# Linear attention with FP32 projections in the two row halves of TensorE and three groups of three tiles a unit

## The chip, the cores and the metric

One core of one Trainium2 chip. The metric is the device time of one execution in microseconds (us), all of it: attention, then two mixture-of-experts stages in the same program. The change touches the attention stage and, in a few lines, the loading that runs beside it.

## The reference, cut to what is computed

```python
def phi(x):                                   # x: 8 batches, 8 heads, 576 tokens, 64
    proj = einsum('bhsd,df->bhsf', x, w_phi)  # w_phi: 64 x 128
    proj = proj - max(abs(proj), axis=-1)
    return concatenate([exp(proj), exp(-proj)], axis=-1)
q_p, k_p = phi(q), phi(k)
kv = einsum('bhsf,bhsd->bhfd', k_p, v)
z = sum(k_p, axis=2)
out = einsum('bhsf,bhfd->bhsd', q_p, kv) / (einsum('bhsf,bhf->bhs', q_p, z) + 1e-6)
x = out as 4608 tokens x 512
x = (sigmoid(x @ moe_w_gate) * (x @ moe_w_val)) @ moe_w_out     # d_ff 1536
x = moe2(x)            # 8 experts with a capacity of 576 tokens each, assigned in order of the logits
```

All inputs and the output are FP32.

## The kernel before, in words

Attention runs over 16 units. A unit is half the heads of a batch, four heads as two pairs of two (`pr` 0 and 1; `hh` is the head within a pair). With 576 tokens a head, a unit has nine tiles of 128 rows: four full tiles for each pair, and one tile in which the last 64 tokens of both pairs share the 128 rows. The host lays q, k and v out like that.

`GROUPS` cuts the nine tiles into five groups: the shared tile alone, and four groups of two tiles. The loop at the end of `attention` runs over steps `tau`, five to a unit; `at` and `once` start a stage of unit `u` at a fixed number of steps after its first, so that several units are under way at once. The order of the lines in that loop is the order in which the instructions stand in each engine's queue; it is written by hand.

The stages of a unit: 
- `load`, `load_v` (L75, L81): DMAs on SP's queue, k four steps and q four steps ahead of their projection.
- `split` (L89 to L92): x is written as a high part, rounded to FP32R, and the rest as a low part; k's high part on ACT, q's on DVE, low parts on POOL and, for k in two groups of five, on DVE.
- `proj` (L101): per tile three FP32R matmuls (high by high, high by low, low by high), with both heads of the pair in the 128 contraction rows against a block-diagonal `w_phi` of 256 columns. One bank holds a group; three banks are in turn.
- `shift` (L118, L119): on DVE, the largest absolute value of each row of 128, and its subtraction, both read from PSUM.
- `k_exp` (L128): two exps on ACT. `kv_mm` (L148): plain FP32 matmuls of v against them, one head in the upper and one in the lower 64 columns of the array. `z_add` (L156 to L162) on POOL and `z_mm` (L167): the sum over tokens.
- `kv_out`, `kv_tr` (L170 to L177): the result out of PSUM and transposed.
- `q_trL`, `q_tr` (L182, L191): transposes of the shifted q; `q_exp` (L198, L200): exps on ACT and a copy on POOL for the shared tile.
- `q_num`, `q_den` (L212, L231), `q_out`, `den_out`: numerators and denominators, out through ACT to DRAM. `recip` inverts the denominators per batch.

Beside this the loop calls `convert`, which for one chunk of the first expert stage's weights at a time loads 64-bit numbers (`win`, 24 chunks of 512 KB) and turns them into FP32 with five DVE instructions (`to_f32`, L319 to L324), one chunk every three steps.

The next stage, `ffn`, starts while attention ends: `START` says at which steps its generator is advanced. Its `in_mm` (L399) and `out_mm` (L421) are the matmuls of the longest stretch of the program. PSUM has eight banks; attention uses three for `pp`, two for `kv`, and one each for `qt`, `nu` and `misc`, the last shared by `kt`, `lt` and `dn`.

Of the kernel before, what the change touches and what calls it, by code (L numbers as in the profile page):

```python
# [29 lines left out]
GROUPS = ((8, 1), (0, 2), (2, 2), (4, 2), (6, 2))  # L30


K_TAGS = ("k", "kh", "kl", "kpm", "kpmL", "kE", "kEL", "z", "v", "vL")
K_TICKS = 5 * NU + 3


def phi_constants(nc, pool, wphi):

    ones = pool.tile([P, 32], F32, tag="ones", bufs=1, name="ones")
    nc.vector.memset(ones, 1.0)  # L40
    w = pool.tile([P, 2 * F], F32, tag="wphi", bufs=1, name="wphi2")
    nc.vector.memset(w, 0.0)
    nc.sync.dma_start(w[0:D, 0:F], wphi)
    nc.sync.dma_start(w[D:P, F:], wphi)
    hi = pool.tile([P, 2 * F], F32R, tag="whi", bufs=1, name="whi")
    lo = pool.tile([P, 2 * F], F32R, tag="wlo", bufs=1, name="wlo")
    nc.vector.tensor_copy(hi, w)
    nc.vector.tensor_tensor(lo, w, hi.bitcast(F32), op=ALU.subtract)
    return hi, lo, ones


def attention(kctx, qctx, tc, K, wphi, qT, kT, vT, num_d, den_d, r_d, units=NU, extra=None):

# [9 lines left out]
    whi, wlo, ones = phi_constants(nc, qp, wphi)  # L63
# [8 lines left out]
    def load(src, tag, u, j):  # L72
        t0, n = GROUPS[j]
        t = T([2 * P], F32, tag, (u, j), 4)
        nc.sync.dma_start(t[:, : n * P], src[u, :, t0 * P : (t0 + n) * P])  # L75

    def load_v(u, j):
        t0, n = GROUPS[j]
        t = T([n, 2, D], F32, "vL" if n == 1 else "v", (u, j), 2 if n == 1 else 5)
        X["v", u, j] = t  # L80
        nc.sync.dma_start(t.rearrange("p n h d -> p (n h d)"), vT[u, :, t0 * P : (t0 + n) * P])  # L81

    def split(tag, u, j):
        n = GROUPS[j][1] * P
        x = X.pop((tag, u, j))[:, :n]
        h = T([2 * P], F32R, tag + "h", (u, j), 4)[:, :n]
        l = T([2 * P], F32R, tag + "l", (u, j), 4)[:, :n]
        if tag == "k":
            A.activation(h, x, AF.Copy)  # L89
        else:  # L90
            V.tensor_copy(h, x)
        (V if tag == "k" and j in (1, 3) else G).tensor_tensor(l, x, h.bitcast(F32), op=ALU.subtract)  # L92

    def proj(tag, u, j):
        n = GROUPS[j][1]
        pp = psk.tile([P, 2, 2, F], F32, tag="pp", bufs=3, name=f"pp{tag}{u}_{j}")
        h, l = X.pop((tag + "h", u, j)), X.pop((tag + "l", u, j))
        for t in range(n):
            c = slice(t * P, (t + 1) * P)
            for i, (x, w) in enumerate(((h, whi), (h, wlo), (l, whi))):  # L100
                PE.matmul(pp[:, t], lhsT=x[:, c], rhs=w, start=i == 0, stop=i == 2)  # L101
        X["pp" + tag, u, j] = pp

    def shift(tag, u, j):

        n = GROUPS[j][1]
        pp = X.pop(("pp" + tag, u, j))
        m = T([2, 2], F32, "m", (tag, u, j), 4)
        if tag == "k":
            pm = T([n, 2, F], F32, "kpmL" if n == 1 else "kpm", (u, j), 1 if n == 1 else 2)  # L110
            X["kp", u, j] = pm
        elif n == 1:
            pm = T([n, 2, F], F32, "qpmL", (u,), 2)
        else:
            if j % 2:
                T([4, 2, F], F32, "qpm", (u, j // 2), 2)
            pm = X["qpm", u, (j - 1) // 2][:, 2 - 2 * (j % 2) : 4 - 2 * (j % 2)]
        V.tensor_reduce(m[:, 0:n], pp[:, 0:n], axis=AX.X, op=ALU.max, apply_absolute_value=True)  # L118
        V.tensor_tensor(pm, pp[:, 0:n], m[:, 0:n, :, None].to_broadcast([P, n, 2, F]), op=ALU.subtract)  # L119

    def k_exp(u, j):
        n = GROUPS[j][1]
        L, bufs = ("L", 2) if n == 1 else ("", 5)
        E = T([n, 2, 2, F], F32, "kE" + L, (u, j), bufs)
        X["E", u, j] = E
        kp = X.pop(("kp", u, j))
        for s in range(2):
            A.activation(E[:, :, :, s, :], kp, AF.Exp, scale=1.0 - 2.0 * s)  # L128

    def kv_mm(u, j):  # L130

        n = GROUPS[j][1]
        pr = max(j - 1, 0) // 2
        rows = slice(64 * pr, 64 * pr + 64)
        first = j in (0, 3)
        if first:
            X["kv", u, pr] = psk.tile([P, 3, P], F32, tag="kv", bufs=2, name=f"kv{u}_{pr}")
        kv = X["kv", u, pr]
        seq = []
        if first:  # L140
            seq.append((X["v", u, 0][rows, 0], X["E", u, 0][rows, 0]))
        if j > 0:
            seq += [(X["v", u, j][:, t], X["E", u, j][:, t]) for t in range(n)]
        for i, (v, E) in enumerate(seq):
            start, stop = first and i == 0, j in (2, 4) and i == len(seq) - 1
            for hh in range(2):
                o = kv[64 * hh : 64 * hh + 64, 0:2].rearrange("p s f -> p (s f)")
                PE.matmul(o, lhsT=v[:, hh], rhs=E[:, hh].rearrange("p s f -> p (s f)"), start=start, stop=stop)  # L148

    def z_add(u, pr, i):  # L150

        E = X["E", u, 2 * pr + 1 + i].rearrange("p t h s f -> p t (h s f)")
        if i == 0:
            rows = slice(64 * pr, 64 * pr + 64)
            z = T([2, 4 * F], F32, "z", (u, pr), 2)
            G.tensor_tensor(z[:, 0], E[:, 0], E[:, 1], op=ALU.add)  # L156
            L = X["E", u, 0].rearrange("p t h s f -> p (t h s f)")
            G.tensor_tensor(z[rows, 0], z[rows, 0], L[rows], op=ALU.add)
        else:
            z = X["z", u, pr]  # L160
            G.tensor_tensor(z[:, 1], E[:, 0], E[:, 1], op=ALU.add)
            G.tensor_tensor(z[:, 1], z[:, 0], z[:, 1], op=ALU.add)  # L162
# [9 lines left out]
    def kv_tr(u, pr):  # L172
        kt = psq.tile([P, 3, P], F32, tag="misc", bufs=1, name=f"kt{u}_{pr}")
# [5 lines left out]
    def q_trL(u):  # L179
        lt = psq.tile([P, 2, P], F32, tag="misc", bufs=1, name=f"lt{u}")  # L180
        for hh in range(2):
            PE.transpose(lt[:, hh], X["qpmL", u][:, 0, hh], ident)  # L182
        e = T([2, 2, P], F32, "eL", (u,), 2)
        for s in range(2):
            A.activation(e[:, s], lt, AF.Exp, scale=1.0 - 2.0 * s)

    def q_tr(u, h):
        pr, hh = h // 2, h % 2
        tp = psq.tile([P, 4, P], F32, tag="qt", bufs=1, name=f"qt{u}_{h}")
        for j in range(4):  # L190
            PE.transpose(tp[:, j], X["qpm", u, pr][:, j, hh], ident)  # L191
# [62 lines left out]
    def at(f, tau, off, n, *pre):  # L254

        u, i = divmod(tau - off, 5)
        if 0 <= u < units and i < n:
            f(*pre, u, i)

    def once(f, tau, off, *post):  # L260
        u, i = divmod(tau - off, 5)
        if 0 <= u < units and i == 0:
            f(u, *post)

    for tau in range(-5, 5 * units + 10):
        at(load, tau, -4, 5, kT, "k")
        at(load, tau, -2, 5, qT, "q")
        at(load_v, tau, -1, 5)
        once(kv_out, tau, 6, 0)
        once(kv_out, tau, 8, 1)  # L270
        at(proj, tau, 0, 5, "k")
        at(kv_mm, tau, 2, 5)
        once(q_den, tau, 13, 1)
        at(shift, tau, 0, 5, "k")
        at(k_exp, tau, 1, 5)
        once(den_out, tau, 13, 1)
        once(q_den, tau, 11, 0)
        once(z_add, tau, 6, 1, 1)
        once(z_add, tau, 4, 0, 1)
        at(q_num, tau, 8, 4)  # L280
        at(split, tau, -2, 5, "k")
        once(q_trL, tau, 5)
        once(kv_tr, tau, 7, 0)
        once(kv_tr, tau, 9, 1)
        once(den_out, tau, 11, 0)
        at(q_out, tau, 8, 4)
        at(q_tr, tau, 6, 4)
        at(proj, tau, 2, 5, "q")
        at(shift, tau, 2, 5, "q")
        at(q_exp, tau, 6, 4)  # L290
        once(z_mm, tau, 5, 0)
        once(z_mm, tau, 7, 1)
        once(z_add, tau, 3, 0, 0)
        once(z_add, tau, 5, 1, 0)
        at(split, tau, 0, 5, "q")
        once(lambda u: recip_load(u // 2) if u % 2 and u + 1 < units else None, tau, 14)
        once(lambda u: recip(u // 2) if u % 2 and u + 1 < units else None, tau, 16)
# [12 lines left out]
def to_f32(nc, pool, src, dst, name):  # L310
# [5 lines left out]
    def rest():  # L316
        lo, hi = w[:, :, 0], w[:, :, 1]
        a = dst.bitcast(I32)
        V.tensor_scalar(a, hi, 0x7FFFFFFF, None, op0=ALU.bitwise_and)  # L319
        af = a.bitcast(F32)  # L320
# [5 lines left out]
    return rest  # L326
# [8 lines left out]
def ffn(ctx, tc, K, num_d, r_d, wos_d, wout, wg2, w1, w2, wlo_d, x2_d, L, free):  # L335
# [178 lines left out]
    def convert(k):  # L514

        while X["conv"] < min(k, NF):
            X.pop(("rest", X["conv"]))()
# [654 lines left out]
def host(inputs):  # L1172
    import numpy as np

    def xT(x):
# [3 lines left out]
        return np.ascontiguousarray(np.concatenate([a, l], axis=2))  # L1179

    def vt(x):
# [3 lines left out]
        return np.ascontiguousarray(np.concatenate([a, l], axis=2)).reshape(NU, P, 9 * P)  # L1185
# [94 lines left out]
```

## Time and profile before

| | us |
|---|---|
| median of three runs | 1867.48 (1866.4 to 1867.83) |
| profiled execution | 1864.9 |
| its span in the trace | 1863.2 |

| engine | busy, us of the span | share |
|---|---|---|
| PE (matmul) | 1791.2 | 96% |
| PEld (weight load) | 1510.1 | 81% |
| DVE | 1317.5 | 71% |
| ACT | 603.3 | 32% |
| POOL | 610.8 | 33% |

Engines: PE is TensorE, PEld its weight loads, DVE VectorE, ACT ScalarE, POOL GpSimd, SP SyncE, whose queue issues most DMAs. A plain FP32 matmul leaves two records on PE, an FP32R matmul one. The duration that a record of PE shows is modelled and runs on into the records behind it, so what a matmul takes of the engine is read from one start to the next. Transposes are matmuls with one record. The line numbers are those of the kernel before.

### The profile page before, as it was taken

What the parts mean: (1) busy time and instruction counts of PE and PEld (TensorE: products, weight loads), DVE (VectorE), ACT (ScalarE), POOL (GpSimd) and SP (SyncE); (2) the same over time, 40 slices, a digit from 0 to 9 for tenths busy, and PEclk for the clock granted to TensorE, in tenths of its full rate; (3) what the DMA queues carried; (4) which work ended last, traced back from release to release, by engine and by line L of the source; (5) the groups of instructions that cost most, each with busy time, mean ns of one, the idle gap of its engine ahead of it and who ended that gap; (6) DMA issues with size and microseconds to landing.
All of it is one profiled execution on the core that took longest, in us unless ns stands there. A gap on an engine that the chain in (4) does not pass through costs nothing.

```text
span 1863.2 us, 33221 instructions
## 1 busy us (share of the span) xinstructions
PE 1791.2 (96%) x11612; PEld 1510.1 (81%) x11612; DVE 1317.5 (71%) x3242; ACT 603.3 (32%) x1256; POOL 610.8 (33%) x589
## 2 busy tenths in 40 slices
PE   7999999998999999999999999999989999999997
PEld 5665666557899999999999999998667888888886
DVE  8999999859786866857758667454767777777410
ACT  4665665562212222221221221111032333233331
POOL 6766777655322223322332222000211102210121
PEclk9999999999999999999999999999989999999999
DMA  4444444427666676666766666110355645564652
GB/s 140 132 131 131 133 137 135 135 66 257 210 216 212 213 239 224 224 232 212 248 223 216 233 219 216 50 54 12 100 171 181 216 145 174 170 214 147 202 179 87
DMA packets 188118, 318.33 MB, mean 171 GB/s; under 512 B 24240, under 2 KB 67504, under 8 KB 187824
## 3 DMA queue, kind: packets, MB, share of 16 engines
q1 hardware_dynamic: 158448, 254.34, 42.9%
q10 hardware_dynamic: 23616, 43.00, 6.1%
q0 software_dynamic: 5888, 18.88, 2.9%
q8 instruction: 92, 1.51, 0.3%
q14 instruction: 74, 0.61, 0.1%
HBM read 244.53 MB, written 71.60 MB: 170 GB/s over the span
## 4 chain that ended last, share of the span: by engine, by line
PE 65%; DVE 6%; DMA 1%; issue 1%; ACT 0%; SPq 0%; POOLq 0%; POOL 0%; DVEq 0%; ACTq 0%
PE pg L399 28%; PE acc L421 14%; PE hp L1080 11%; PE yp L1114 8%; PE yr L1101 1%; PE tp L1053 1%; PE cnt L801 1%; DMA rb<-r_d 1%; DVE cmp L780 1%; DVE junk L479 1%; DVE oa L987 0%; DMA xg<-x_d,idx 0%; PE lg L455 0%; DVE xl L376 0%; PE num_ix L996 0%
## 5 line engine op out<-in xcount | busy, mean ns | idle before, releaser
L399 PE MATMUL pg<-xl,wh 128*128 128x384 f32 x1152 | 389.5, 338 | 0.9 <-DVE xl L376 0.9
L399 PE MATMUL pg<-xh,wl 128*128 128x384 f32 x1152 | 388.1, 337 | 1.1 <-POOL wl L387 1.1
L399 PE MATMUL pg<-xh,wh 128*128 128x384 f32 x1152 | 387.0, 336 | 0.1
L547 POOL TENSOR_TENSOR el<-er,eh 128x512 fp32r<-128x512 f32 x128 | 182.3, 1424 | 469.2 <-ACT eh L546 431.3
L402 ACT ACTIVATE sg<-pg 128x384 f32<-128x384 f32 x144 | 70.7, 491 | 530.5 <-PE pg L399 514.5
L408 DVE TENSOR_TENSOR sg<-sg,pg 128x384 f32<-128x384 f32 x132 | 72.9, 552 | 228.1 <-PE pg L399 217.3
L399 PEld LDWEIGHTS pg<-xh,wh 128*128 128x128 f32 x1152 | 217.2, 189 | 8.1 <-issue 0.9
L399 PEld LDWEIGHTS pg<-xh,wl 128*128 128x128 f32 x1152 | 215.9, 187 | 6.7 <-POOL wl L387 1.3
L399 PEld LDWEIGHTS pg<-xl,wh 128*128 128x128 f32 x1152 | 216.4, 188 | 1.3 <-DVE xl L376 1.3
L479 DVE SCALAR_TENSOR_TENSOR junk<-x,wg 128x512 f32<-128x512 f32 x240 | 202.1, 842 | 5.5
L421 PE MATMUL acc<-wh,gh 128*128 128x512 f32 x396 | 159.5, 403 | 4.9 <-DVE gh L415 2.7
L421 PE MATMUL acc<-wh,gl 128*128 128x512 f32 x396 | 158.3, 400 | 1.8 <-DVE gl L416 1.7
L421 PE MATMUL acc<-wl,gh 128*128 128x512 f32 x396 | 157.6, 398 | 2.3 <-POOL wl L437 2.2
L1114 PE MATMUL yp<-wh,hh 128*128 128x512 f32 x256 | 108.2, 423 | 0.0
L546 ACT ACTIVATE eh<-er 128x512 fp32r<-128x512 f32 x128 | 81.0, 633 | 75.9 <-POOL el L547 42.4
L1114 PE MATMUL yp<-wh,hl 128*128 128x512 f32 x256 | 100.2, 391 | 0.0
L1114 PE MATMUL yp<-wl,hh 128*128 128x512 f32 x256 | 100.1, 391 | 0.0
L128 ACT ACTIVATE kE<-kpm 128x512 f32<-128x512 f32 x128 | 73.9, 630 | 71.4 <-DVE kpm L119 67.6
L1087 DVE SCALAR_TENSOR_TENSOR hl<-hp,hh 128x288 fp32r<-128x288 f32 (+1 forms) x128 | 54.0, 421 | 60.3 <-ACT hh L1085 60.1
L1080 PE MATMUL hp<-xhT,wh 128*128 128x288 f32 x512 | 94.0, 305 | 0.6 <-ACT xhT L1055 0.5
L1080 PE MATMUL hp<-xhT,wl 128*128 128x288 f32 x512 | 94.3, 301 | 0.0
L421 PEld LDWEIGHTS acc<-wh,gl 128*128 128x128 f32 x396 | 75.0, 190 | 22.3 <-DVE gl L416 4.7
(281 smaller groups left out, 3722.6 us busy)
## 6 DMA issues: line engine op xcount, KB each, us to landing
er<-in_w_dram SPq DMA_DIRECT2D x128, 256.0 KB
wlo_d<-el ACTq DMA_DIRECT2D x128, 256.0 KB
wr<-in_w_dram SPq DMA_DIRECT2D x128, 256.0 KB
wl<-wlo_d SPq DMA_DIRECT2D x128, 256.0 KB
wh<-wos_d SPq DMA_DIRECT2D x120, 256.0 KB
wl<-wos_d SPq DMA_DIRECT2D x120, 256.0 KB
dbli<-in_win_dram SPq DMA_DIRECT2D x24, 512.0 KB
num_d<-nums SPq DMA_DIRECT2D x32, 288.0 KB
```

What stands on the lines that cost most here:

```text
L128: A.activation(E[:, :, :, s, :], kp, AF.Exp, scale=1.0 - 2.0 * s)
L399: PE.matmul(pg, lhsT=a[:, cc], rhs=b, start=c == 0 and j == 0, stop=c == 3 and j == 2)
L402: A.activation(T([TB], F32, "sg", (g,)), X.pop(("pg", g, 0)), AF.Sigmoid)
L408: V.tensor_tensor(u, sg, X.pop(("pg", g, 1)), op=ALU.mult)
L421: PE.matmul(X["acc", i][t], lhsT=a[:, c], rhs=b, start=f == 0 and j == 0, stop=f == NF - 1 and j == 2)
L479: V.scalar_tensor_tensor(junk, x, 1.0, X["wg"][:, e], op0=ALU.mult, op1=ALU.mult, accum_out=out)
L546: A.activation(h, r, AF.Copy)
L547: G.tensor_tensor(tile("el", F32R, k - 1, 3), r, h.bitcast(F32), op=ALU.subtract)
L780: V.tensor_tensor(t[:, c], d[:, c, None, :].to_broadcast([P, NC // 4, NT, 2]), K["it2"][:, None, 0:P:4].to_broadcast([P, NC // 4, NT, 2]), ...
L1080: PE.matmul(hp, lhsT=x[:, cc], rhs=y[:, c, s], start=c == 0 and j == 0, stop=c == 3 and j == 2)
L1087: V.scalar_tensor_tensor(hl[:, s], hs, 0.0, hh[:, s].bitcast(F32), op0=ALU.max, op1=ALU.subtract)
L1114: PE.matmul(yp, lhsT=x[:, cc], rhs=y, start=f == 0 and j == 0, stop=f == 7 and j == 2)
```

## The change

- A unit has three groups of three tiles (`GT`), the shared tile first; the host puts it first too. The loop has three steps a unit, and its lines stand in a new order.
- The splits are gone. `proj` multiplies FP32 by FP32: for each tile two matmuls, one per head, with 64 contraction rows each, head 0 in the upper and head 1 in the lower half of the array's rows. The two heads write to two banks. `pp` has two banks for k and two for q, one set of each.
- `shift` and `k_exp` work on three tiles at once (768 elements a row).
- `kv` has a bank for each pair, which `kt` shares; `lt` shares the bank of `qt`, `dn` that of `nu`. `misc` is gone.
- Loads come two steps ahead of their use, in three DMAs a unit for each of k, q and v.
- `to_f32` gives its five instructions in two parts, three and two, which run one step and two steps after the load; a chunk is started at every second step. `START` and `K_TICKS` are recounted.

```diff
-GROUPS = ((8, 1), (0, 2), (2, 2), (4, 2), (6, 2))
-K_TICKS = 5 * NU + 3
+GT = 3
+K_TICKS = 3 * NU + 2
...
     def load(src, tag, u, j):
+        nc.sync.dma_start(T([GT * P], F32, tag, (u, j), 3), src[u, :, j * GT * P : (j + 1) * GT * P])
...
+    def proj(tag, u, j):
+        pp = psk.tile([P, 2, 512], F32, tag="pp" + tag, bufs=1, name=f"pp{tag}{u}_{j}")
+        x = X.pop((tag, u, j))
+        for t in range(GT):
+            for hh in range(2):
+                r = slice(hh * D, (hh + 1) * D)
+                PE.matmul(pp[:, hh, t * F : (t + 1) * F], lhsT=x[r, t * P : (t + 1) * P], rhs=w[r], start=True, stop=True)
...
+        V.tensor_reduce(m, pp, axis=AX.X, op=ALU.max, apply_absolute_value=True)
+        pm = pm.rearrange("p t h f -> p h t f")
+        V.tensor_tensor(pm, pp, m[:, :, :, None].to_broadcast([P, 2, GT, F]), op=ALU.subtract)
...
+        todo = [[(0, t, slice(0, P)) for t in (1, 2)], [(0, 0, slice(0, P)), (0, 1, slice(0, P))], []][j]
+        if j == 0:
+            todo.insert(0, (0, 0, slice(0, D)))
+        else:
+            todo += [(1, t, slice(0, P)) for t in ((2,) if j == 1 else range(GT))]
+        if j == 1:
+            todo.append((1, None, slice(D, P)))
...
-        kt = psq.tile([P, 3, P], F32, tag="misc", bufs=1, name=f"kt{u}_{pr}")
+        kt = psq.tile([P, 3, P], F32, tag=f"kv{pr}", bufs=1, name=f"kt{u}_{pr}")
...
-        dn = psq.tile([P, 288], F32, tag="misc", bufs=1, name=f"dn{u}_{pr}")
+        dn = psq.tile([P, 288], F32, tag="nu", bufs=1, name=f"dn{u}_{pr}")
...
+    for tau in range(-2, 3 * units + 6):
+        at(load, tau, -2, kT, "k")
+        at(load, tau, 0, qT, "q")
+        at(load_v, tau, -1)
+
+        once(q_out, tau, 7, 2)
+        once(den_out, tau, 6, 0)
+        once(den_out, tau, 8, 1)
+        once(kv_out, tau, 3, 0)
+        once(kv_out, tau, 5, 1)
+
+        once(q_trL, tau, 3)
+        once(q_tr, tau, 4, 0)
+        once(q_tr, tau, 5, 2)
+        once(q_expL, tau, 3)
+        once(q_exp, tau, 4, 0)
+        once(q_exp, tau, 5, 2)
+        at(proj, tau, 0, "k")
+        at(proj, tau, 2, "q")
+        at(shift, tau, 0, "k")
+        at(shift, tau, 2, "q")
+        once(kv_tr, tau, 3, 0)
+        once(kv_tr, tau, 5, 1)
+        once(q_tr, tau, 4, 1)
+        once(q_tr, tau, 5, 3)
+        once(q_exp, tau, 4, 1)
+        once(q_exp, tau, 5, 3)
+        once(z_add, tau, 1, 0, 0)
+        once(z_add, tau, 2, 0, 1)
+        once(z_add, tau, 3, 1, 0)
+        once(z_add, tau, 3, 1, 1)
+
+        once(q_num, tau, 5, 0)
+        once(q_num, tau, 6, 1)
+        once(q_num, tau, 7, 3)
+        once(q_out, tau, 5, 0)
+        once(q_out, tau, 6, 1)
+        once(q_out, tau, 7, 3)
+        at(kv_mm, tau, 1)
+        once(q_num, tau, 6, 2)
+        at(k_exp, tau, 0)
+
+        once(z_mm, tau, 2, 0)
+        once(z_mm, tau, 4, 1)
+        once(q_den, tau, 5, 0)
+        once(q_den, tau, 7, 1)
...
+    def one():
...
+    def two():
...
-START = (K_TICKS - 8, K_TICKS, K_TICKS, K_TICKS + 1, K_TICKS + 3)
+START = (K_TICKS - 5, K_TICKS, K_TICKS, K_TICKS + 1, K_TICKS + 2)
...
-        if late and tau % 3 == 2:
+        if late:
             late.pop(0)()
-        if tau >= 3 and tau % 3 == 0 and todo:
+        if tau >= 0 and tau % 2 == 0 and todo:
...
+            late.extend(to_f32(nc, cv, win[:, f, s], K["win_raw"][f, s], f"i{f}_{s}"))
```

## Rows read from the trace of the kernel before

**Rows 1.** The page's 40 slices: busy tenths of each engine, and the granted clock.

```profile
PE   7999999998999999999999999999989999999997
DVE  8999999859786866857758667454767777777410
PEclk9999999999999999999999999999989999999999
```

**Rows 2.** Windows of three units together: length, busy time of each engine, clock, DMA.

```profile
core 0: us, PE busy (x) PEld busy (x) DVE busy (x) ACT busy (x) POOL busy (x), PEclk, DMA share, GB/s
200.00:273.20 73.20, 68.85 (x602) 44.69 (x595) 68.06 (x111) 45.20 (x105) 52.74 (x61) 1.00 0.44 135
```

**Rows 3.** The same view, of a stretch with a lower clock.

```profile
179.50:186.40 6.90, 6.89 (x38) 3.32 (x38) 3.60 (x8) 3.19 (x8) 2.90 (x6) 0.56 0.13 38
```

**Rows 4.** Weight loads of `q_trL`: duration min/median/max in ns, first and last start.

```profile
L182 PEld LDWEIGHTS lt<-ident,qpmL x32: 137/140/143, 20.1 to 391.9; 128*128 128x128 f32 x32
```

**Rows 5.** Timeline of PE, 213 to 220 us: start, length, line, tile, shapes, records.

```profile
214.39 0.55 PE L176 MATMUL kt<-ident,kvf 128*128 128x128 f32 x3
214.77 0.60 PE L191 MATMUL qt<-ident,qpm 128*128 128x128 f32 x4
215.13 0.37 PE L101 MATMUL ppq<-whi,qh 128*128 128x256 f32 x1
215.33 0.28 PE L101 MATMUL ppq<-wlo,qh 128*128 128x256 f32 x1
...
216.16 0.28 PE L101 MATMUL ppk<-whi,kl 128*128 128x256 f32 x1
```

**Rows 6.** The same view, about 206.7 to 210.3 us.

```profile
206.75 0.28 PE L101 MATMUL ppk<-whi,kl 128*128 128x256 f32 x1
206.96 1.08 PE L148 MATMUL kv<-kE,v 128*64 128x256 f32 x8
207.98 1.18 PE L231 MATMUL dn<-qE,KV 128*32 128x288 f32 x16
209.09 1.19 PE L212 MATMUL nu<-qE,KV 128*64 128x288 f32 x8
```

**Rows 7.** Waits of PE, 200 to 273.2 us: total us, times, longest.

```profile
PE ppq L101 <- DVE kpm L119: 1.5, 2, 0.8
...
PE ppk L101 <- DVE qh L91: 0.4, 1, 0.4
```

**Rows 8.** Groups by shape on DVE, 200 to 273.2 us: busy us, mean ns | idle before.

```profile
L119 DVE TENSOR_TENSOR kpm<-ppk,mk 128x512 f32<-128x512 f32 x12 | 8.3, 692 | 0.8
...
L118 DVE TENSOR_REDUCE mk<-ppk 128x4 f32<-128x512 f32 x12 | 8.1, 678 | 0.0
...
L119 DVE TENSOR_TENSOR kpmL<-ppk,mk 128x256 f32<-128x256 f32 x3 | 1.3, 424 | 0.1
L118 DVE TENSOR_REDUCE mk<-ppk 128x2 f32<-128x256 f32 x3 | 1.3, 417 | 0.0
```

**Rows 9.** Windows of tile `win` alone, then of `wo`, converted behind attention.

```profile
200.00:273.20 73.20, 22.74 (x25) 0.00 (x0) 0.00 (x0) 1.00 0.44 135
...
417.00:502.00 85.00, 39.00 (x60) 7.48 (x12) 14.41 (x11) 0.96 0.68 220
```

**Rows 10.** Groups by shape on ACT and POOL, 200 to 273.2 us.

```profile
L128 ACT ACTIVATE kE<-kpm 128x512 f32<-128x512 f32 x24 | 13.9, 631 | 12.1 <-DVE kpm L119 11.5 <-POOL qE L198 0.5
...
L128 ACT ACTIVATE kEL<-kpmL 128x256 f32<-128x256 f32 x6 | 2.2, 409 | 4.8 <-DVE kpmL L119 4.8
...
L156 POOL TENSOR_TENSOR z<-kE 128x512 f32<-128x512 f32 x7 | 9.6, 1374 | 0.0
```

**Rows 11.** Timeline of all engines at the start, and of PE at attention's end.

```profile
2.68 1.53 SPq L75 DMA_DIRECT2D k<-in_kT_dram  x3
...
5.09 0.58 PE L101 MATMUL ppk<-whi,kh 128*128 128x256 f32 x1 [5.09 <-DVE wlo L48]
...
414.81 1.18 PE L231 MATMUL dn<-qE,KV 128*32 128x288 f32 x16
```

More of the change, by code (lines that the diff above doesn't have):

```diff
@@ L40, in phi_constants @@
     nc.vector.memset(ones, 1.0)
[L41 to L49, printed above, removed]
+    w = pool.tile([P, F], F32, tag="wphi", bufs=1, name="wphi2")
+    for hh in range(2):
+        nc.sync.dma_start(w[hh * D : (hh + 1) * D], wphi)
+    return w, ones
 def attention(kctx, qctx, tc, K, wphi, qT, kT, vT, num_d, den_d, r_d, units=NU, extra=None):
@@ L83, in split @@
[L83 to L92, printed above, removed]
-    def proj(tag, u, j):
[L95 to L101, printed above, removed]
+        t = T([GT, 2, D], F32, "v", (u, j), 4)
@@ L130, in kv_mm @@
     def kv_mm(u, j):
[L132 to L143, printed above, removed]
@@ L144, in kv_mm @@
-        for i, (v, E) in enumerate(seq):
-            start, stop = first and i == 0, j in (2, 4) and i == len(seq) - 1
+        v, E = X["v", u, j], X["kE", u, j]
+        todo = [[(0, t, slice(0, P)) for t in (1, 2)], [(0, 0, slice(0, P)), (0, 1, slice(0, P))], []][j]
+        if j == 0:
+            todo.insert(0, (0, 0, slice(0, D)))
[3 more added lines that the diff above has]
+            todo.append((1, None, slice(D, P)))
@@ L146, in kv_mm @@
+        for i, (pr, t, r) in enumerate(todo):
+            start = (j, i) == (0, 0) or (j, i) == (1, 2)
+            stop = (j, i) == (1, 1) or (j, i) == (2, GT - 1)
+            if start:
+                X["kv", u, pr] = psq.tile([P, 3, P], F32, tag=f"kv{pr}", bufs=1, name=f"kv{u}_{pr}")
+            v1, E1 = (X["v", u, 0][r, 0], X["kE", u, 0][r, 0]) if t is None else (v[r, t], E[r, t])
             for hh in range(2):
-                o = kv[64 * hh : 64 * hh + 64, 0:2].rearrange("p s f -> p (s f)")
@@ L148, in kv_mm, with e @@
-                PE.matmul(o, lhsT=v[:, hh], rhs=E[:, hh].rearrange("p s f -> p (s f)"), start=start, stop=stop)
+                o = X["kv", u, pr][64 * hh : 64 * hh + 64, 0:2].rearrange("p s f -> p (s f)")
+                PE.matmul(o, lhsT=v1[:, hh], rhs=E1[:, hh].rearrange("p s f -> p (s f)"), start=start, stop=stop)
     def z_add(u, pr, i):
-        E = X["E", u, 2 * pr + 1 + i].rearrange("p t h s f -> p t (h s f)")
+        def e(j, t):
+            return X["kE", u, j][:, t].rearrange("p h s f -> p (h s f)")
@@ L252, in recip, with at @@
         nc.sync.dma_start(r_d[:, b * S : (b + 1) * S].rearrange("h (c i) -> h c i", i=36), rr)
[L254 to L258, printed above, removed]
+    def at(f, tau, off, *pre):
+        u, j = divmod(tau - off, 3)
+        if 0 <= u < units:
+            f(*pre, u, j)
     def once(f, tau, off, *post):
-        u, i = divmod(tau - off, 5)
-        if 0 <= u < units and i == 0:
+        u, j = divmod(tau - off, 3)
+        if 0 <= u < units and j == 0:
@@ L263, in once @@
             f(u, *post)
[L265 to L297, printed above, removed]
@@ new lines, in attention @@
+    for tau in range(-2, 3 * units + 6):
[40 more added lines that the diff above has]
+        once(q_den, tau, 7, 1)
+        once(lambda u: recip_load(u // 2) if u % 2 and u + 1 < units else None, tau, 9)
+        once(lambda u: recip(u // 2) if u % 2 and u + 1 < units else None, tau, 11)
@@ L516, in convert @@
         while X["conv"] < min(k, NF):
-            X.pop(("rest", X["conv"]))()
+            for step in X.pop(("rest", X["conv"])):
+                step()
             X["conv"] += 1
```

71 lines of the change are left out of this document (29 added, 42 removed).

## The prediction

> **What bounds the kernel now.** I read the 40 slices of the page first [rows 1]: DVE is at eight to nine tenths for the first eight slices and PE close to ten tenths, then DVE falls and PE stays. A slice is 46.6 us, so the attention stage is the first 415 us or so, and only there are two engines full at once. Everything the diff touches lies in that stage, apart from a few lines at the hand-over to the next one (below).
>
> Next, the windows of three undisturbed units of the steady state [rows 2]: in 73.2 us PE is busy 68.85, DVE 68.06, POOL 52.74 and ACT 45.20; per unit that is 22.95 of 24.4 for PE and 22.7 for DVE. So both are within 7% of the unit. The waits of PE there [rows 7] are five rows of 4.3 us in sum, 1.4 a unit, mostly on DVE's shift: PE is kept from its own 23.0 by DVE. The reader is to see that speeding one of the two alone would gain 1.4 us a unit at most; the change has to shorten both.
>
> The mean unit comes from the first and last start of `q_trL`, 20.1 and 391.9 us [rows 4]: 15 units in 371.8, 24.79 each. That is above 24.4 because in two places PE waited for DVE and was then granted a lower clock: in one stretch of 6.9 us the granted clock is 0.56, mostly the 1.2 GHz level [rows 3].
>
> **PE, part by part.** A projection of one tile takes three records now, at a pitch of 0.118 us (215.33 to 216.16 is seven pitches [rows 5]). A unit has nine tiles for k and nine for q: 54 records, 6.4 us. These go.
>
> In their place come 18 tiles with two matmuls each, one per head, in plain FP32 with 64 rows. The FP32 matmuls of before show what plain FP32 costs: `kv_mm` has two records per matmul, and 8 records of 256 columns in two column strips last 1.02 us [rows 6], four steps of about a quarter of a microsecond for 256 columns, so a record streams 256 columns in about 0.23 once the mode change (below) is taken off. A record of 128 columns should take half. The rows of that size are the transposes: seven records of 128 columns, each with its own weight load of 128 columns, from 214.39 to 215.13 [rows 5], 0.106 each. A tile has 2 heads by 2 records.
> - Side by side (the two halves of the array at once): 2 x 0.106 a tile, 18 tiles, 3.8 us a unit.
> - In series: 4 x 0.106 a tile, 7.6 us a unit, more than the 6.4 removed.
>
> No row of before has two matmuls in different row halves at once. The nearest are those in column strips: `q_den` has 16 records in four strips and takes 1.11 us (207.98 to 209.09), and `q_num` has 8 records of the same 288 columns in two strips and takes as long (1.18 and 1.19 us in their rows), so the records of different strips do run together [rows 6]. Each head writes a bank of its own, as the strips write partitions of their own. I take 3.8 and keep 7.6 as the other end.
>
> A rule of the Trainium skill speaks against this. "TensorE: Matmul & The Clock Gate", Part 3, The mechanism, says that a weight load overlaps a matmul in flight only when the row group differs; then the second pass of a head would load after the first had streamed, a tile would take the series price, and the sum would be that of the first rival. The transposes disagree: at a pitch equal to their stream they load the same rows every time. The same page measures four row tiles at 3.07 times one; if two lost as much (an estimate), the projections would cost 4.9 and the total 17 us more.
>
> Changes of tile mode: between the last projection (206.75 plus one pitch) and `kv_mm` at 206.96 lie 0.09 us [rows 6]. Counted in the code, a unit changes mode 20 times before and 17 after: 0.3 less. `kv_mm`, `q_num`, `q_den`, `z_mm` and the transposes keep their number and size. PE needs 22.95 - 6.4 + 3.8 - 0.3 = 20.05 us a unit.
>
> **DVE.** The q casts and the low parts of k leave it. The ops read from PSUM grow from 512 to 768 elements: 678 and 417 ns for 512 and 256 give 0.94 us for a reduce of 768, 692 and 424 give 0.96 for a subtract [rows 8]; three of each for k and for q make 11.4 us. The conversions of `win`, 24 in 48 steps, are 1.5 a unit: 4.55 us each in the steady state (22.74 for 25 instructions, five to a conversion) and 3.25 after attention, beside less POOL work [rows 9], so 4.9 to 6.8. With the reciprocal DVE needs 16.6 to 18.5, under PE's 20.05 at both ends: it stops being a bound, and costs the sum nothing. Its cover is thin, though: at most 3.8 us.
>
> **ACT and POOL.** ACT loses the k copies. Its exps of 768 elements should cost 0.85 (631 and 409 ns at 512 and 256 [rows 10]), so the six of a unit 5.1 where they were 5.3; ACT comes to 15.1 a unit. POOL loses `ql` and `kl` and keeps eight z additions of 1.37 [rows 10] and four copies, 12.5. Both hide under PE.
>
> **Waits from single banks.** `pp` has one pair of banks for k and one for q, and `kt`, `lt` and `dn` now share banks with `kv`, `qt` and `nu`. I walked the new order with these durations; a step of three tiles is 5.6 to 7.4 us on PE. Ahead of `proj` of the next step the shift has ended by some 2 us. The second `q_num` of a step stands behind `kv_mm` (1.3 us), which covers `q_out` (0.41). The second `q_tr` of a step waits for the two exps of the first (1.2 us), and these for what ACT has queued; projections of 1.4 us and in one step `kv_tr` lie between. There I find 0.1 to 0.2 us of wait in two of three steps, 0.35 a unit. z additions end over 2 us before `z_mm`. Unit: 20.4 us.
>
> **Loads and SP.** The loads come two steps ahead, 13.7 us, where the first k load took from 2.68 to a product at 5.09 [rows 11]; nine loads a unit replace fifteen, with the same bytes. The `win` load is one step ahead (6.8 us) instead of two of the short ones (9.8); the shifts of 3.8 us stand before its first use on DVE. I put no cost on this; if that cover failed, DVE would stop ahead of the next shift, and PE would feel it once DVE's slack of 1.9 to 3.8 us a unit is used up.
>
> **Ends.** The first `q_trL` is at 20.1. Without splits, with the same first product near 5 and steps 0 to 2 led by DVE (shifts, exps, then `kv_mm`), I walk it to 17.0: 3.1 earlier. From the last `q_trL` to the end of `q_den` are 24.0 us now (391.9 to 414.81 plus 1.1 [rows 6, 11]), with 24 matmuls of the next stage inside; the five new steps come to 23.2. The stage behind moves as a block: its start is tied to the end of the loop, its own conversions run with the same instructions, so it gives nothing.
>
> **Sum.** 15 x (24.79 - 20.4) = 65.9, plus 3.1 and 0.8, is 69.8. The profiled execution has 1864.9, so 1795.1; the median of the runs lies 2.6 above it (1867.48), so 1798. With waits between none and the 1.4 of now, and 4 us either way at the ends, this case reaches from 1784 to 1817.
>
> **Rivals.**
> - The halves of the array run in series (the change then doesn't do what it says). PE needs 7.6 instead of 3.8: unit 24.2, 15 x 0.59 + 3.9 = 12.8 saved, 1855. For it: no row of before shows row halves at once. Against: the strips of rows 6. The weight-load rule above would end here too. Chance 0.15.
> - ACT's order takes the gain back. If the two exps of k (1.7 us) come ahead of those of q, a second `q_tr` waits 1.7 + 1.2 less the cover of 1.4 or 1.8: 1.5 and 1.1, some 2.8 a unit with latency; unit 22.85, 1835. For it: the single `qt` bank, and ACT takes its queue in the program's order. Against: ACT has 5 us a unit free. Chance 0.16.
> - Slower: each change between the halves drains like a change of mode. In series, and with 36 changes of 0.094 a unit (3.4 us), the unit is 27.6, 15 x 2.81 less 3.9 is 38 lost: 1906. It decides from 0.47 us a tile on (the unit is then 25.05), against 0.21 forecast and 0.42 in series. Chance 0.07. The Trainium skill, "TensorEngine Tiling (Array Packing)", Key Properties, says that changing the mode drains the engine and changing only the tile doesn't; the 0.09 us of rows 6 agree with the first half, no row shows the second.
>
> **How the numbers follow.** My forecast has 0.60, the rivals 0.15, 0.16 and 0.07; 0.02 is left for the rest. A measurement of this kernel can tell about 0.2%, so faster means below 1863.7: the forecast, the ACT case and nearly all of the series case, 0.90; within 0.2%: 0.04, the top of the series case; slower 0.06. The range goes from 1780, a little below the best of my case, to 1857, which takes in the ACT case and half of the series case.
>
> **What would show it.** Right: `q_trL` starts 20 to 21 us apart; records of the two heads' projections start together, and a group of three tiles takes about 0.65 us on PE; the waits of PE for DVE nearly gone; DVE near nine tenths. Series: a group takes 1.3 us and more. ACT case: PE waits at `qt` for `qE`. What would make me wrong besides: the clock falling to 1.2 GHz in the thin first steps and staying there, or DVE's conversions growing over 6.8 us a unit.

## The result, and the profile after

| | before, us | after, us |
|---|---|---|
| median | 1866.94 (four runs, 1864.91 to 1867.83) | 1818.84 (four runs, 1814.72 to 1819.88) |
| ratio | | 0.974 (0.9722 to 0.9757) |
| profiled execution, its span | 1864.9, 1863.2 | 1814.72, 1813.0 |

The change made the kernel 48 us faster. The forecast was 1798, 70 us faster: the time lies in the stated range (1780 to 1857), though just above the 1784 to 1817 that the prediction gave its own case; the sign is right, and about a third of the expected gain did not come. Both profiled executions are the fastest of their four, and the shortfall is split on their traces: 69.8 forecast, 50.2 found between the two spans.

The 40 slices of the page of after, which answer to [rows 1]. A slice is 45.3 us, attention is the first 8.

```profile
PE   7999999899999999999999999999989999999997
DVE  7999998788768567686776855736757776777410
POOL 5555555444122223222233221001112211210221
PEclk8999999999999999999999999999989999999999
```

At this resolution nothing tells what went wrong: PE is full, DVE full as well. DVE was to be "near nine tenths" and to "stop being a bound"; five slices of nine tenths or more fit the first and say nothing of the second. What DVE costs is only seen unit by unit. The weight loads of `q_trL`, with first and last start, answer to [rows 4]:

```profile
L159 PEld LDWEIGHTS lt<-ident,qpm x32: 138/142/143, 18.7 to 336.1; 128*128 128x128 f32 x32
```

From 18.71 to 336.05 are 15 units of 21.16 us on average, where 24.79 were before and 20.4 forecast. But no unit is 21.16 long. Nine take 19.88, six take 22.1 to 23.9. Windows of one long unit, of the short one behind it, and of a stretch within the long one, which answer to [rows 2] and [rows 3] (length, busy us of each engine, granted clock, DMA):

```profile
core 0: us, PE busy (x) PEld busy (x) DVE busy (x) ACT busy (x) POOL busy (x), PEclk, DMA share, GB/s
81.69:104.95 23.26, 21.70 (x221) 13.99 (x217) 22.60 (x24) 13.33 (x26) 12.77 (x13) 0.93 0.31 102
104.95:124.83 19.88, 19.88 (x221) 12.66 (x217) 18.04 (x21) 13.33 (x26) 12.84 (x13) 1.00 0.66 203
...
89.80:93.20 3.40, 3.40 (x28) 3.15 (x28) 3.37 (x3) 1.08 (x2) 3.23 (x4) 0.53 0.52 194
```

In the short unit PE is busy for the whole 19.88 us and DVE for 18.04, both as forecast (20.05 and 16.6 to 18.5). In the long one the same 221 instructions of PE take 3.4 us more: DVE is busy for 22.60 of 23.26, PE stands still for 1.56 and then runs 3.4 us at about half the granted clock (0.53, nearly all of it the 1.2 GHz level). All the waits of PE from the first to the last `q_trL`, which answer to [rows 7] (total us, times, longest), are one row:

```profile
PE qt L172 <- DVE qpm L96: 12.3, 8, 2.8
```

So `q_tr` waits for the shift of q. Where DVE is at that time, the timeline of DVE, POOL and PE in the long unit shows (start, length, line, tile):

```profile
81.23 1.27 POOL L133 TENSOR_TENSOR z<-kE 128x512 f32<-128x512 f32 x1 [4.23 <-ACT kE L102]
81.25 1.53 DVE L317 TENSOR_SCALAR win<-dbli 128x512 int32<-128x512 int32 x1
...
82.58 1.34 POOL L134 TENSOR_TENSOR z<-z,kE 64x512 f32<-64x512 f32 x1
82.82 1.38 DVE L318 TENSOR_SCALAR win<-win 128x512 f32<-128x512 f32 x1
...
84.00 1.33 POOL L138 TENSOR_TENSOR z<-kE,kE 128x512 f32<-128x512 f32 x1
...
84.23 1.38 DVE L319 TENSOR_SCALAR win<-win 128x512 int32<-128x512 int32 x1
...
88.44 0.96 DVE L96 TENSOR_TENSOR qpm<-ppq,mq 128x768 f32<-128x768 f32 x1
...
89.45 0.44 PE L172 MATMUL qt<-ident,qpm 128*128 128x128 f32 x2 [1.56 <-DVE qpm L96]
89.82 1.49 PE L81 MATMUL ppk<-wphi,k 64*128 64x128 f32 x12
...
91.10 1.50 PE L81 MATMUL ppq<-wphi,q 64*128 64x128 f32 x12
```

Three instructions of one conversion of `win` and the z additions of POOL go one for one: each DVE instruction takes about as long as the POOL addition beside it, 1.38 to 1.53 us, where one alone takes 0.43 (L317 over the whole program: 0.416 at the least, 0.432 in the median). The three take 4.29 instead of about 1.3, the shifts behind them in DVE's queue come 3 us late, and the q shift that ends at 89.40 is what PE has been waiting for. Behind the wait the 12 records of a projection take 1.28 us to the next group (89.82 to 91.10), where they take 0.77 at the full clock.

The rows that answer to [rows 8] to [rows 10], by shape in the short unit (busy us, mean ns):

```profile
L323 DVE SCALAR_TENSOR_TENSOR win<-dbli,win 128x512 int32<-128x512 int32 x2 | 3.3, 1644 | 0.1
L96 DVE TENSOR_TENSOR qpm<-ppq,mq 128x768 f32<-128x768 f32 x3 | 2.9, 958 | 0.1
...
L94 DVE TENSOR_REDUCE mk<-ppk 128x6 f32<-128x768 f32 x3 | 2.9, 953 | 0.6 <-PE ppk L81 0.5
...
L317 DVE TENSOR_SCALAR win<-dbli 128x512 int32<-128x512 int32 x2 | 0.9, 457 | 0.0
```

The shift costs what was worked out for 768 elements (0.94 and 0.96). The conversions don't: over the whole loop a conversion takes 5.56 us of DVE, 8.3 a unit, where 3.25 to 4.55, or 4.9 to 6.8 a unit, was taken.

Last, the matmuls of three tiles, which answer to [rows 5]:

```profile
98.17 0.94 PE L81 MATMUL ppk<-wphi,k 64*128 64x128 f32 x12
98.94 0.84 PE L81 MATMUL ppq<-wphi,q 64*128 64x128 f32 x12
99.71 0.55 PE L153 MATMUL kt<-ident,kvf 128*128 128x128 f32 x3
```

A group takes 0.77 us (98.17 to 98.94 to 99.71): the two heads do run side by side.

### The profile page after: what moved, and what is told of

Its sections match the earlier page's. It is cut to its first block, busy times and chain, and to the rows that moved or that the text cites. A ratio compares the mean times of both kernels' runs of the same rounds, so it can differ in the third digit from the quotient of the medians.

```text
span 1813.0 us, 32696 instructions
## 1 busy us (share of the span) xinstructions
PE 1747.5 (96%) x11900; PEld 1477.1 (81%) x11900; DVE 1270.3 (70%) x2999; ACT 577.1 (32%) x1112; POOL 525.3 (29%) x461
## 3 DMA queue, kind: packets, MB, share of 16 engines
q8 instruction: 94, 1.54, 0.3%
## 4 chain that ended last, share of the span: by engine, by line
PE 69%; DVE 4%; DMA 1%; issue 1%; ACT 0%; SPq 0%; POOLq 0%; DVEq 0%; ACTq 0%
PE pg L398 30%; PE acc L420 15%; PE hp L1080 12%; PE yp L1114 8%; PE yr L1101 1%; PE tp L1053 1%; PE cnt L801 1%; DVE cmp L780 1%; DMA rb<-r_d 0%; DMA xg<-x_d,idx 0%; PE lg L454 0%; PE warm L670 0%; PE num_ix L996 0%; DVE oa L987 0%; DMA wos_d<-wh 0%
## 5 line engine op out<-in xcount | busy, mean ns | idle before, releaser
L478 DVE SCALAR_TENSOR_TENSOR junk<-x,wg 128x512 f32<-128x512 f32 x240 | 194.5, 810 | 5.6
L420 PEld LDWEIGHTS acc<-wh,gh 128*128 128x128 f32 x396 | 75.3, 190 | 17.9 <-issue 3.5
```

Source lines behind the costliest of these rows:

```text
L420: PE.matmul(X["acc", i][t], lhsT=a[:, c], rhs=b, start=f == 0 and j == 0, stop=f == NF - 1 and j == 2)
L478: V.scalar_tensor_tensor(junk, x, 1.0, X["wg"][:, e], op0=ALU.mult, op1=ALU.mult, accum_out=out)
```

## The experiments

### Without the conversions

```diff
-            late.extend(to_f32(nc, cv, win[:, f, s], K["win_raw"][f, s], f"i{f}_{s}"))
+            to_f32(nc, cv, win[:, f, s], K["win_raw"][f, s], f"i{f}_{s}")
+            k = 2 * f + s
+            nc.sync.dma_start(K["win_raw"][f, s], w1[k // 8, :, k % 8])
```

> The changed kernel without the five DVE instructions of each conversion of `win`; the 512 KB load of each chunk stays, and the chunk's tile is filled by a further DMA of 256 KB from `w1`, so the first expert stage works with other weights. Theory: six of fifteen units are 22.1 to 23.9 us long instead of 19.88, because DVE's conversions, drawn out beside POOL's z additions, make the shift of q late for the transposes at the head of the next step; without them every unit is 19.9, the wait of `qt` for `qpm` is gone, and the time falls by 15 to 20 us, to about 1797. Rival 1, loads that land late: with half as many bytes again in DMA the long units stay or grow. Rival 2, TensorE's granted clock falls by itself and the waits follow from it: long units stay.

1793.44 us, a little below what was expected. The windows view from 60 to 300 us, here and in after:

```profile
60.00:300.00 240.00, 240.00 (x2608) 152.85 (x2606) 138.71 (x158) 161.34 (x315) 133.99 (x147) 1.00 0.57 180
```

```profile
60.00:300.00 240.00, 230.50 (x2445) 146.84 (x2447) 221.76 (x230) 150.34 (x293) 139.87 (x136) 0.98 0.47 147
```

PE is busy without a gap and never below the full clock; every unit from the second on takes 19.9, the first 17.8. From the first to the last `q_trL` are 296.24 us against 317.34 in after: the conversions cost PE 21.1 us there. More DMA traffic (180 against 147 GB/s) did no harm, so a transfer is not the cause. Whether it is the conversions by themselves or their meeting with POOL, this run leaves open.

### With two z additions a unit instead of eight

```diff
-            G.tensor_tensor(z[:, 0], e(*a), e(*b), op=ALU.add)
-            G.tensor_tensor(z[r, 0], z[r, 0], e(0, 0)[r], op=ALU.add)
...
-            G.tensor_tensor(z[:, 1], z[:, 0], z[:, 1], op=ALU.add)
```

> The changed kernel with two z additions a unit instead of eight (the denominators leave most of the sum out), so that POOL works about 4 us a unit instead of 12. Theory (conversions are drawn out by POOL): a conversion takes 2.7 to 3.3 us where it took 5.5 on average, every unit is 19.9, the time falls by 15 to 20 us. Rival: the conversions are too much for DVE by themselves, whatever POOL does: they stay near 5 us, and the long units stay.

1792.45 us, with all the conversions in. The windows view of the same stretch, of all work and of tile `win` alone (DVE, ACT, POOL):

```profile
60.00:300.00 240.00, 240.00 (x2606) 152.80 (x2604) 200.60 (x248) 161.37 (x315) 45.95 (x74) 1.00 0.51 160
```

```profile
60.00:300.00 240.00, 64.84 (x90) 0.00 (x0) 0.00 (x0) 1.00 0.51 160
```

18 conversions of 3.60 us (2.7 to 3.3 were expected); PE has no gap. DVE is still busy for 84% of the time and does no harm. This run keeps most of DVE's work, the one before nearly all of POOL's (133.99 of 139.87 us), and both lose the long units; behind the first `acc`, a matmul of the next stage, they take 1435.6 and 1433.7 us where after takes 1435.2, so the gain lies in attention. With the two runs the cause is settled: not POOL's load as such, nor a DVE that is merely busy, but that the two coincide.

### The shift of q ahead of that of k

```diff
-        at(proj, tau, 0, "k")
         at(proj, tau, 2, "q")
-        at(shift, tau, 0, "k")
+        at(proj, tau, 0, "k")
         at(shift, tau, 2, "q")
+        at(shift, tau, 0, "k")
```

> The changed kernel with the projection and the shift of q ahead of those of k in each step; all work stays. Theory (the order on DVE is at fault: the shift of q, which the next step's first transposes need, stands last before the conversions): the shift of q ends 1.9 us earlier, the waits of `qt` for `qpm` (9.5 us) go to under 2, units 19.9 to 20.3, about 1803. Rival: DVE is full in sum (11.4 of shifts, 8.3 of conversions, 0.5 of others are 20.2 us a unit, over PE's 19.9), so the waits move to `ppk` or `ppq` and the mean unit stays at 20.5 to 21.2, 1808 to 1819.

1801.32 us (1798.44 to 1803.03), ratio 0.965 (0.9634 to 0.9667). Every unit but the first takes 20.2; a conversion now takes 2.7 to 2.9 us, since it mostly falls where POOL has no z addition. So the order of q and k within a step decides how often the two engines meet. PE gets a new wait of about 0.2 us a unit, from 20 to 321 us:

```profile
PE qt L172 <- ACT qE L181: 4.8, 16, 1.6
```

### That, and the exps of k one step later

```diff
+        at(k_exp, tau, 1)
...
-        at(k_exp, tau, 0)
```

The new line stands behind `once(q_exp, tau, 5, 2)`; the rest is as in the run before.

> The kernel of the third experiment (q ahead of k), and the exps of k moved one step on, behind the first exps of q on ACT. In the third experiment the unit is 20.2, with 0.35 us of wait of `qt` for `qE`, once a unit, because the exps of k (1.6 us) stand ahead of those of q on ACT. If that order is the cause, the wait goes and the unit is 19.9, the time 1796 to 1798. Rival: what comes later for it (`z`, `kv`) is then late in its turn: the unit stays at 20.2 or grows, with waits of PE for `kE` or `z`.

1792.72 us (1791.2 to 1794.21), ratio 0.9618 (0.9602 to 0.9634). Units of 20.05. The windows of all work and of `win`:

```profile
60.00:300.00 240.00, 238.89 (x2590) 151.75 (x2586) 211.01 (x247) 151.93 (x312) 141.45 (x144) 1.00 0.50 157
```

```profile
60.00:300.00 240.00, 74.42 (x90) 0.00 (x0) 0.00 (x0) 1.00 0.50 157
```

A conversion takes 4.13 us here, so a good part of the meetings is back, and yet no unit is long: this order bears them, with the shift of q, which PE needs soonest, first in DVE's queue of a step. (The run before had the same order of shifts and fewer meetings, and does not tell the two apart.) The wait for `qE` is gone, as expected, but a unit falls only from 20.15 to 20.05. The rest of the time gained lies in the first unit (18.4 against 22.1 us) and behind the first `acc` (1430.3 against 1437.0), which this edit doesn't explain.

### The last z addition one step later

```diff
-        once(z_add, tau, 3, 1, 1)
+        once(z_add, tau, 4, 1, 1)
```

> The changed kernel with the last pair of z additions one step later, so that no step has four of them (two, four and two become two with four copies fewer; the step after the first gets the pair). If the burst of four additions in the first step of a unit is what draws out the conversions that stand there, the long units go down from six to three or fewer and the time to 1800 to 1808. Rival: the collisions depend on POOL's total alone (12 us a unit), which stays: as many long units, 1813 to 1820.

1826.41 us (1821.94 to 1831.26), ratio 0.9804 (0.9782 to 0.9826): slower than after, against both expectations. From the sixth on every unit takes 21.3 to 22.6, a conversion 6.1 us, and PE waits in nearly every unit, from 60 to 300 us:

```profile
PE qt L172 <- DVE qpm L96: 11.5, 12, 1.1
PE kv L144 <- POOL z L139: 2.1, 4, 0.5
```

The edit did not spread POOL's work, though. In after the three steps of a unit have four, two and two additions; the moved pair lands on the pair of the next step, so they now have two, four and two. In the trace the four start at 216.50, 217.85, 219.41 and 221.20, and the next pair follows at 223.68 and 225.03. So the burst came one step later, and the conversions were drawn out further. Whether additions spread evenly would part the two engines was not run.

### Both heads in the upper half of the rows

```diff
-                r = slice(hh * D, (hh + 1) * D)
+                r = slice(0, D)
```

> The changed kernel with both heads' projections in the upper half of the array's rows (head 1 is computed from head 0's rows); instructions, shapes and banks stay. If the halves run side by side because they are halves, a group of three tiles goes from 0.77 to about 1.4 us, the unit to 23.7 to 24, and the time to 1855 to 1862. If plain FP32 with 64 rows has that price by itself, 0.77 stays.

1869.83 us, beside 1865.16 for the kernel before. Units of 23.95 and no waits; a group of three tiles:

```profile
153.44 1.60 PE L81 MATMUL ppk<-wphi,k 64*128 64x128 f32 x12
154.88 1.50 PE L81 MATMUL ppq<-wphi,q 64*128 64x128 f32 x12
```

1.44 us, twice 0.77 less 0.1. Without the two halves plain FP32 takes back all that the rest of the change gains. The time is above what was expected because the ends are longer: the first `q_trL` comes at 25.4 us (18.7 in after), and from the last one to the first `acc` of the next stage are 43.7 (41.75).

### Half by half: three tiles of head 0, then three of head 1

```diff
-        for t in range(GT):
-            for hh in range(2):
+        for hh in range(2):
+            for t in range(GT):
```

> The changed kernel with the projections of a group issued head by head (three tiles in the upper half, then three in the lower) instead of alternating. If TensorE takes matmuls in queue order and only neighbours in different halves overlap, a group goes from 0.77 to about 1.3 us and the unit to 23.5 or so, the time to 1855; if each half takes its own matmuls out of the queue ahead, 0.77 and 1815 to 1819 stay.

1813.5 us. The expectations gave full series or full overlap; two groups take 1.86 us (154.02 to 155.88), 0.93 each, between 0.77 and 1.44. At the seam of two groups only records of different halves overlap (those with start times within 0.01 us):

```profile
154.02 1.04 PE L81 MATMUL ppk<-wphi,k 64*128 64x128 f32 x10
154.79 0.27 PE L81 MATMUL ppq<-wphi,q 64*128 64x128 f32 x1
154.90 0.27 PE L81 MATMUL ppk<-wphi,k 64*128 64x128 f32 x1
154.90 0.27 PE L81 MATMUL ppq<-wphi,q 64*128 64x128 f32 x1
...
155.88 0.66 PE L172 MATMUL qt<-ident,qpm 128*128 128x128 f32 x4
```

So PE does run records of the other half ahead, but only a few; the alternation in the source is needed. The units behind the first are all 20.9, 1.0 above 19.88, without waits, and the time is no worse than that of after, whose long units cost more than this.

### The new order with the old split projections

```diff
+        h = T([GT * P], F32R, tag + "h", (u, j), 2)
+        l = T([GT * P], F32R, tag + "l", (u, j), 2)
...
+            for i, (x, w) in enumerate(((h, whi), (h, wlo), (l, whi))):
+                PE.matmul(pp[:, t], lhsT=x[:, c], rhs=w, start=i == 0, stop=i == 2)
...
+        at(split, tau, -1, "k")
...
+        at(split, tau, 1, "q")
```

> The changed kernel's order, groups and banks, but with the projections of before: FP32R in three matmuls a tile, with the splits on ACT, DVE and POOL (two of nine tiles' buffers fewer). It parts the projection from the regrouping. If the projection is what made the gain: PE needs 6.4 where it needs 4.6 now, a unit of 21.7 to 22; DVE gets 3.5 us more, 21.7 and over with more POOL work beside it; the unit comes to 22.5 to 25 and the time to 1840 to 1870. If regrouping and order made it, the unit stays near 21 and the time near 1815.

1841.36 us, units of 22.47 on average. This parts the change in two: regrouping and the new order take the mean unit from 24.79 to 22.47, plain FP32 in the halves takes it to 19.88 where nothing waits, 21.16 in after. So neither branch of the expectation holds alone. The time has more in it than the units: the first `q_trL` is at 27.3 us, 8.6 later than in after. From 60 to 300 us PE is busy for 236.85 of 240 us and DVE for 191.06.

### Other banks for the last unit's numerators and denominators

```diff
-        nu = psq.tile([P, 288], F32, tag="nu", bufs=1, name=f"nu{u}_{i}")
+        nu = psq.tile([P, 288], F32, tag="qt" if (u, i) == (units - 1, 2) else "nu", bufs=1, name=f"nu{u}_{i}")
...
-        dn = psq.tile([P, 288], F32, tag="nu", bufs=1, name=f"dn{u}_{pr}")
+        dn = psq.tile([P, 288], F32, tag="kv0" if u == units - 1 else "nu", bufs=1, name=f"dn{u}_{pr}")
```

> The kernel after, with other banks for the last unit alone: q_den of that unit takes kv0's bank, and its third q_num takes qt's, so that no matmul of the tail waits for ACT to empty the one bank that nu and dn share. In the kernel after PE waits 5.2 us for ACT between 345 and 363 us, and the last q_trL to the end of the last q_den takes 27.0 us where 23.2 were forecast. Theory (the shared bank and ACT's queue with its wh copies and its table load make those 3.8 us): the waits at nu and dn for nums and den fall below 1.5 us in sum, the last q_trL to the end of the last q_den takes 22.5 to 24, and the span shortens by 2 to 4 us: 1811 to 1817 beside 1814.7 to 1819.9. Rival A (the stage behind is held by something else, as POOL's wl or its loads): the tail shortens as well but the first acc does not come earlier, and the time stays. Rival B (the forecast's walk is short, PE simply needs more): waits go and others take their place, the tail stays near 27.

> The version with q ahead of k and k_exp a step later, with the same banks for the last unit as the run before this. There the last q_trL to the end of the last q_den takes 26.8 us (317.68 to 343.33 plus 1.1) and PE waits 4.2 us at nu and dn for ACT. Theory: 22.5 to 24 and 2 to 4 us less, 1787 to 1791 beside 1791.2 to 1794.2. Rival A: the tail shortens and the time stays. Rival B: the tail stays near 27.

The second pair looks at the end of attention. In after, the timeline there reads:

```profile
351.09 2.18 ACT L385 ACTIVATE wh<-win 128x512 fp32r<-128x512 f32 x4
...
351.25 1.18 PE L212 MATMUL dn<-qE,KV 128*32 128x288 f32 x16 [0.56 <-ACT nums L199]
...
353.62 1.19 PE L193 MATMUL nu<-qE,KV 128*64 128x288 f32 x8 [1.20 <-ACT den L217]
...
360.24 1.19 PE L193 MATMUL nu<-qE,KV 128*64 128x288 f32 x8 [1.40 <-ACT nums L199]
```

`nu` and `dn` have one bank; to give it back ACT must copy it out, and ACT is then at the weight copies of the next stage. With the other banks the same matmuls follow one another, and of 5.2 us of waits on ACT from 345 us on 1.3 are left:

```profile
354.60 1.18 PE L212 MATMUL dn<-qE,KV 128*32 128x288 f32 x16
355.70 2.16 PE L193 MATMUL nu<-qE,KV 128*64 128x288 f32 x16
...
360.08 1.19 PE L193 MATMUL nu<-qE,KV 128*64 128x288 f32 x8
```

The last `q_trL` to the end of the last `q_den` takes 21.75 us (340.55 to 361.20 plus 1.1) instead of 27.0, and 22.1 instead of 26.8 in the better order; to the first `acc` of the next stage it is 36.5 and 36.8, where without the edit it is 41.75 and 41.5. The theory holds, and the tail came out shorter than expected.

In the whole time this is harder to see. The kernel after with these banks: 1810.3 us (1804.56 to 1819.51), ratio 0.9694 (0.968 to 0.9707), less than the 0.974 of after, but the difference of some 8 us is more than the tail's 5, and its long units fall otherwise (its profiled execution is the slowest of the six, with a mean unit of 21.5). The better order with them: 1791.14 us (1790.62 to 1793.61), ratio 0.9594 (0.9581 to 0.9607), an interval that touches that without (0.9602 to 0.9634). In the two traces of that pair the first `acc` comes 4.2 us earlier (355.0 against 359.2), and the spans are 1789.4 and 1789.5: what lies behind took 4.1 us longer. Over all the kernels here what lies behind the first `acc` runs from 1430 to 1441 us, though only attention was edited. So the tail's gain is shown up to the next stage; how much of it reaches the end stays open. By its median this is the fastest version that computes the whole, 4.1% below the kernel before.

## Why the prediction was right, and where it was short

The shortfall of 69.8 less 50.2, by the parts of the sum, each from the two profiled executions:

| part | forecast gain | found | short |
|---|---|---|---|
| 15 units: 24.79 to 20.4; to 21.16 | 65.9 | 54.5 | 11.4 |
| first `q_trL`: 20.13 to 17.0; to 18.71 | 3.1 | 1.4 | 1.7 |
| last `q_trL` to first `acc`: 36.7 to 35.9; to 41.75 | 0.8 | -5.0 | 5.8 |
| all behind the first `acc`: 1434.6; 1435.2 | 0 | -0.6 | 0.6 |

**PE's need.** Right in the number, in part by luck. 20.05 us were forecast, 19.88 is a unit in which PE has no gap. Two errors cancel. A group takes 0.77 (0.65 was forecast), six of them 4.6 a unit instead of 3.8. And the projections of before took more than was taken off: from one start to the next their 54 records take 7.8 us a unit (200 to 273.2 us), not 6.4, since the first and the last record of each run of them take 0.21, as from 215.13 to 215.33 in [rows 5]. The rest of a unit is 15.15 before and 15.3 after, where the sum had 16.25. The sum comes as near with other projections: 23.85 for both heads in one half (found 23.95), 22.65 for the split ones (22.47).

**Side by side or in series.** Right, and the two experiments on the halves show why. Records of one half follow at 0.12 us (1.44 for 12), those of two halves start together. The price of "in series" was nearly right, 1.44 a group against 1.27, and the kernel that pays it is no faster than before, where 1855 was forecast. By the rule of the Trainium skill that was weighed ("TensorE: Matmul & The Clock Gate", Part 3, The mechanism: a weight load overlaps a matmul in flight only in another row group) the series price was to be paid in after; it isn't, and in one half, with the same row group throughout, the pitch of 0.12 leaves no room for an uncovered load either (the records of these loads last 0.19 on PEld).

**DVE.** This is the step that failed. The prediction said that DVE "stops being a bound, and costs the sum nothing", from a conversion at 3.25 to 4.55 us, and counted the waits at 0.35 a unit on ACT's account. The conversion took 5.56, because the price was taken as a mean of rows with more and with less POOL work; it is no mean but two prices, 0.42 to 0.69 an instruction alone and 1.38 to 1.80 beside a z addition, and which one is paid depends on where in the step the two fall. Nor does the mean alone make the long units: DVE is busy for 19.55 us a unit in after (293.24 in 15), under PE's 19.88, and in the better order conversions of 4.13 hurt nothing (whether that order would bear 5.56 was not run). What hurts is three drawn-out instructions ahead of the shift of q. Of the signs that were named, "the waits of PE for DVE nearly gone" failed, with 12.3 us, and with it "`q_trL` starts 20 to 21 us apart". That the cover is thin was said, and that conversions over 6.8 us a unit would make the prediction wrong; they took 8.3. The price is 21.1 us of units against the run without conversions. Without conversions, with two z additions, and in the better order, where no unit behind the first is long, the time is 1792 to 1793, below the forecast.

**The clock.** A term put at nothing, and wrongly. The forecast carried no fall after a wait, though [rows 3] show one, and the trace of before has three between its first and last `q_trL` (at 28.6, 178.8 and 329.0 us), not two. In after four of the eight waits are followed by a stretch at about half the granted clock: those of 1.56, 2.17 and 2.18 us by 3.4 us, like the one above, and the one of 2.8 us in the first unit by 10.3 us from 25 us on (0.51 in the windows view). Two of 1.54 and 1.56 and two of 0.25 us are followed by none. Half of these 20.5 us, about 10 (an estimate), is lost to the clock, so about half of the 21.1; the other half is the waiting itself, 12.3 us in after and 1.5 without the conversions. The long unit above bears this out: it is 3.4 us longer than the short one, 1.8 by the wait (87.46, where `q_tr` begins in that trace, to 89.45, less two pitches of 0.11) and 1.6 by the stretch.

**ACT's order.** The rival fell: in steady state PE never waits for ACT in after, and so the forecast's own 0.35 a unit was not there either. The exps cost 0.84 as forecast; ACT is busy for 13.33 a unit, not 15.1, from which the copies of k had not been taken off. The wait came only when q was put first, at 0.2 us a unit.

**Waits from single banks.** In the loop right, none decides. At the end wrong: the walk gave 23.2 us to the end of `q_den` where it took 27.0, because it did not put ACT's copies for the next stage between `nu` and `dn`. The experiment with other banks gives 21.75. Besides, 12 matmuls of the next stage (2.1 us at a pitch of 0.174) that stood ahead of the last `q_den` before stand behind it now, which makes the 5.8 of the table out of 3.8.

**The first `q_trL`.** 1.7 late. The projections there run at half pace until about 14.5 us (1.44 a group), then at 0.77, and `q_trL` waits 0.8 for the shift of q. In the fastest version they are at 0.77 from 13.11 on, and its first `q_trL` starts at 17.20; in the same order with the old banks the half pace lasts until about 16 us, and it starts at 18.66. The windows show the granted clock as 1.00 there, but the traces hold no record of it before 14.9, 13.1 and 16.6 us in these three, so what it was until then is open; the walk took the full pace.

**Loads.** Right: no wait for a load in the loop.

**The range.** The low end of its own case is summed wrongly: with units of 20.05 and 4 us at the ends it is 1788.5, not 1784. Nothing hangs on it.

## What to carry to other kernels

Where DVE and POOL work on SBUF at the same time, cost each DVE instruction at two prices, alone and beside POOL, and ask what stands behind it in DVE's queue; a mean hides both. Put what the bound engine needs soonest first in that queue: here that order bore conversions of 4.13 us, where moving a pair of additions by a step drew them out to 6.1. And reckon with the clock: half of what the waits cost here came behind them. When a bank serves two results in turn, look at what else the engine that empties it has queued at the ends of the loop, not only in its middle.

## What the runs showed of the hardware

- DVE instructions that read only SBUF and POOL additions took turns one for one: 0.42 us became 1.38 to 1.53 for the most part, 0.69 became 1.64 to 1.80, while POOL's additions went only from 1.27 to 1.33 for the most part, at most 1.8. DVE's shifts, which read PSUM, took 0.95 to 0.96 beside POOL or not. The Trainium skill, "SBUF — State Buffer", Who interferes with whom, has a rule for this: the two engines share a port pair that the first holds for its whole instruction, and a DVE instruction with at most one SBUF input, outside the two-port modes, stays out of it. The rows agree for the instructions with two SBUF inputs (L322, L323) and for the shifts; for those with one (L317 to L319) they agree if these run in a two-port mode, which no row shows.
- In after, waits of PE of 1.56, 2.17 and 2.18 us were followed by 3.4 us at about half the granted clock (0.53), one of 2.8 by 10.3 us (0.51). Two of 1.54 and 1.56 were followed by none.
- Plain FP32 with 64 rows and 128 columns: three tiles of two heads take 0.77 us with the halves alternating, 0.93 with three of one half ahead of three of the other (two groups in 1.86), 1.44 in one half.
